# A fused attention and gated feed-forward kernel: two more warm-up products, later masks, small norm steps on GpSimd, and a new order table

## The chip, the cores and the metric

One core of one Trainium2 chip. The metric is device microseconds (us) of one execution, measured in repeated runs; a separate profiled execution gives the trace. All runs quoted are of the state that the records call fast, and a kernel is compared with the kernel before on the same chip in the same rounds. In what follows a "product" is one matmul instruction of TensorE, and "the clock" is the pace of TensorE, which is half or full here (427 or 216 ns for a product of 512 columns).

## The reference

Two blocks with pre-normalisation on x of 2048 x 1024, all in bf16:

```python
h  = x + A(layernorm(x))          # 32 heads of 32; q, k, v, o projections of 1024 x 1024
h2 = h + B(layernorm(h))          # gate and up 1024 x 3584, silu(gate) * up, down 3584 x 1024
# A runs over 4 segments of 512 rows: causal softmax inside a segment, mixed by sigmoid(beta)
# with a linear memory M, z that is carried from segment to segment:
o = g * (phi(q) @ M) / (phi(q) @ z + 1e-6) + (1 - g) * softmax(q k^T * scale + mask) @ v
M = M + phi(k)^T v ;  z = z + sum(phi(k))
```

## The kernel before

The program lists all operations with their data dependences, runs a model of the core over them, and emits each engine's instructions in the order that the model found. Where two operations are ready, class and place in the list decide; a table shifts these per "stage" (a counter that the code advances at each group of operations).

```python
SHIFT = { 0: (-19, 0), 1: (424, -1), 2: (293, 0),   # ... cut: 482 entries, the last one 491
          488: (-337, 0), 489: (-203, 1), 490: (159, -1), 491: (-10, 0), }
...
    def schedule(self):
        for o in ops:
            late, cls = SHIFT.get(o.unit, (0, 0))
            o.seq += late + 1e-6 * o.seq
            o.cls += cls
...
    def warm(self, n, deps=()):                       # n products of zeros, 512 columns each
        w = self.oT[0][:, 4, :]
        o = self.mms(gr, [(... self.oT[0][:, 4, 0:128], w, True, True, 512)] * n, 0, split=n)
        o.cost["pe"] *= 2
...
    def constants(self):
        self.dve_op(lambda e: e.memset(w, 0.0), 300.0, [], [w], 0)
        self.warm(10)
        ...                                           # cut: identity, ones
        P(lambda e: e.memset(b, 0.0), 128, [], [b], 3)        # masks: 2 on GpSimd
        P(lambda e: e.memset(hm, 0.0), 4, [], [hm], 3)
        for j in range(4):                                    # and 8 on the vector engine
            self.dve_op(lambda e, bj=bj: e.memset(bj, 1.0), 180, [], [bj], 3)
            self.dve_op(lambda e, hj=hj: e.memset(hj, 1.0), 150, [], [hj], 3)
...
    def first_tile(self, t):                          # t = 0..3; odd tiles: sums on ScalarE
        var, mean, op = self.ln_act(t, x) if t % 2 else self.ln_stats(
            t, x, 1, (self.applied,) if t else ())
        self.dve_op(lambda e: e.tensor_scalar(ve, var, self.EPS, None, op0=ALU.add), ...)
        self.g.op("pool", 570.0, ... e.tensor_tensor(rs, ve, mh, op=ALU.pow) ...)
        for b in range(2):                            # two half tiles
            self.applied = self.dve_op(... e.tensor_scalar(xb, xb, mean, rs, op0=op, op1=ALU.mult) ...)
            self.transposes(...)                      # 4 products with the identity, TensorE
            self.evac(gr, out, ..., engs=("dve", "act"))      # out of PSUM, into xnT
...
    def first_half(self):     # loads, in this order: x tiles 0, 1; half of wq; x tiles 2, 3; half of wk; ...
        ...                   # then the four first_tile, then products of 128 columns per tile
```

The up-projection loads its weights in blocks of 512 KB into two pairs of buffers (w1b, w3b); a block's load starts when TensorE has read the block two before it.

The softmax here doesn't subtract the row's maximum and nothing guards it: scores larger than these inputs give would overflow.

## Time and profile before

| | us |
|---|---|
| first three runs | 906.48, 907.34, 907.40 |
| profiled run (span) | 905.84 (904.1) |
| all 37 runs of this study, several chips and calls | mean 906.4, from 904.5 to 909.8 |

In a page, line 1 of each part is the busy time of an engine. In the list of waits a row is "who waited <- for whom: us in total, times, longest". In the timeline a row is start, length, engine, line, operation, tiles and shapes, count, and in brackets the idle time just before it with what ended it. TensorE is busy 99% of the span, so only its idle time and its pace are to be won. The lines stand in the prediction.

### The profile page before, as it was taken

The numbers are of one execution on the slowest core, as the hardware profiler recorded it, in microseconds if no ns is written. First come the engines' busy times: TensorE is split into PE (matmuls) and PEld (weight loads), VectorE is DVE, ScalarE is ACT, GpSimd is POOL, SyncE is SP. The second block draws the span as 40 slices with busy tenths as digits, with TensorE's granted clock in tenths as the row PEclk, the third lists the DMA queues.
The fourth block names the chain that finished last, engine by engine and source line by source line (L and its number), as shares of the span: only waits on it lengthen the run. The fifth ranks groups of instructions, "written<-read, shape, count | busy, mean of one in ns | idle before, by whom it ended". The sixth has DMA issues, their size and how long they took to land.

```text
span 904.1 us, 12979 instructions
## 1 busy us (share of the span) xinstructions
PE 897.7 (99%) x5559; PEld 409.7 (45%) x5559; DVE 427.7 (47%) x653; ACT 284.5 (31%) x303; POOL 186.7 (21%) x246
## 2 busy tenths in 40 slices
PE   8999999999999999999999999999999999999998
PEld 6444444434444344444444444444444444444445
DVE  5667749688785765545434222201343333431111
ACT  5767757685866721111111110000121111110000
POOL 2446537465562732000000000000000000000000
PEclk9999999999999999999999999999999999999999
DMA  7896962653551257455215022013123221301110
GB/s 236 207 242 191 246 153 79 164 163 86 151 115 48 77 198 224 93 155 139 70 59 163 24 72 68 24 47 94 47 76 93 70 61 56 94 24 41 36 40 30
DMA packets 146473, 96.27 MB, mean 106 GB/s; under 512 B 45424, under 2 KB 133616, under 8 KB 146416
## 3 DMA queue, kind: packets, MB, share of 16 engines
q1 hardware_dynamic: 146416, 95.45, 38.3%
q8 instruction: 44, 0.72, 0.3%
q14 instruction: 13, 0.11, 0.0%
HBM read 76.55 MB, written 8.39 MB: 94 GB/s over the span
## 4 chain that ended last, share of the span: by engine, by line
PE 97%; DMA 2%; DVE 0%; issue 0%; ACT 0%; POOL 0%; SPq 0%
PE ps L702 90%; PE ps L1076 4%; PE ps L1031 3%; DMA w3b<-in_B_w_dram 1%; DMA wp<-in_A_wq_dram 1%; DMA xs<-in_A_x_dram 0%; PE ps L714 0%; DVE lnst L825 0%; ACT xnT L725 0%; POOL rstd L852 0%; DVE xs L856 0%; DVE ob L1225 0%; DVE lnmv L828 0%; DVE lnve L850 0%; DVE blkmask L788 0%
## 5 line engine op out<-in xcount | busy, mean ns | idle before, releaser
L702 PE MATMUL ps<-hnT,w1b 128*128 128x512 bf16 x896 | 220.0, 379 | 0.0
L702 PE MATMUL ps<-hnT,w3b 128*128 128x512 bf16 x896 | 219.0, 379 | 0.9 <-DMA w3b<-in_B_w_dram 0.9
L1193 ACT ACTIVATE sg<-ps 128x512 bf16<-128x512 f32 x112 | 66.9, 597 | 426.5 <-PE ps L702 426.5
L702 PE MATMUL ps<-w2b,hm 128*128 128x512 bf16 (+1 forms) x924 | 198.2, 373 | 0.0
L1196 DVE SCALAR_TENSOR_TENSOR t<-sg,ps 128x512 bf16<-128x512 bf16 x112 | 76.8, 685 | 198.9 <-ACT sg L1193 198.5
L1043 ACT ACTIVATE et<-ps 128x2048 bf16<-128x2048 f32 x80 | 150.0, 1875 | 39.7 <-PE ps L1031 39.2
L702 PEld LDWEIGHTS ps<-w2b,hm 128*128 128x128 bf16 x924 | 90.4, 98 | 103.2
L702 PEld LDWEIGHTS ps<-hnT,w1b 128*128 128x128 bf16 x896 | 87.2, 98 | 105.7 <-issue 7.9
L702 PEld LDWEIGHTS ps<-hnT,w3b 128*128 128x128 bf16 x896 | 86.7, 98 | 106.8 <-DMA w3b<-in_B_w_dram 2.2
L1052 POOL TENSOR_SCALAR_AFFINE_SELECT et<-et 128x512 bf16<-128x512 bf16 x96 | 88.4, 927 | 81.7 <-ACT et L1043 81.6
L1201 DVE SCALAR_TENSOR_TENSOR hm<-t,ps 128x512 bf16<-128x512 bf16 x112 | 76.3, 685 | 43.3 <-PE ps L702 40.6
L1225 DVE TENSOR_TENSOR ob<-hr,ps 128x512 bf16<-128x512 bf16 (+1 forms) x33 | 22.0, 670 | 125.0 <-PE ps L702 125.0
L702 PE MATMUL ps<-wo,oT 128*128 128x512 bf16 x256 | 63.9, 380 | 0.0
L702 PE MATMUL ps<-xnT,wp 128*128 128x512 bf16 (+1 forms) x352 | 62.5, 326 | 0.7 <-ACT xnT L725 0.5
L702 PE MATMUL ps<-hnT,wp 128*128 128x512 bf16 x256 | 62.6, 380 | 0.0
L702 PEld LDWEIGHTS ps<-xnT,wp 128*128 128x128 bf16 x352 | 28.8, 100 | 26.6 <-issue 2.8
L835 POOL TENSOR_SCALAR lnve<-lnmv 128x1 f32<-128x1 f32 x28 | 6.3, 228 | 150.8 <-DVE lnmv L828 150.7
L702 PEld LDWEIGHTS ps<-wo,oT 128*128 128x128 bf16 x256 | 23.9, 98 | 29.4 <-issue 2.7
L702 PEld LDWEIGHTS ps<-hnT,wp 128*128 128x128 bf16 x256 | 23.3, 98 | 28.5 <-issue 3.8
L1130 DVE STREAM_TRANSPOSE R<-Rc 128x1024 f32<-128x1024 f32 (+1 forms) x32 | 34.7, 1096 | 0.1
L1135 POOL TENSOR_TENSOR R<-Nsb,R 128x512 f32<-128x512 f32 x20 | 26.7, 1341 | 34.9 <-DVE R L1130 26.7
L1165 DVE TENSOR_TENSOR h<-h,ps 128x512 bf16<-128x512 bf16 x32 | 21.9, 684 | 24.8 <-PE ps L702 24.7
(85 smaller groups left out, 594.3 us busy)
## 6 DMA issues: line engine op xcount, KB each, us to landing
w3b<-in_B_w_dram SPq DMA_DIRECT2D x28, 512.0 KB, 3.8
w1b<-in_B_w_dram SPq DMA_DIRECT2D x28, 512.0 KB, 3.8
wp<-in_A_wv_dram SPq DMA_DIRECT2D x8, 1024.0 KB, 5.3
wp<-in_A_wq_dram SPq DMA_DIRECT2D x7, 1024.0 KB, 5.1
wp<-in_A_wk_dram SPq DMA_DIRECT2D x7, 1024.0 KB, 6.0
w2b<-in_B_w_dram SPq DMA_DIRECT2D x7, 1024.0 KB, 6.2
xs<-in_A_x_dram SPq DMA_DIRECT2D x16, 256.0 KB, 5.6
h<-in_A_x_dram SPq DMA_DIRECT2D x16, 256.0 KB, 3.7
```

Source lines behind the costliest of these rows:

```text
L702: return [e.matmul(p[0](gr), p[1], p[2], start=p[3], stop=p[4]) for p in part]
L1031: ins.append(e.matmul(self.bank(gr, j, 512 - 128 * kc, off), k[r, g0 + g, 128 * kc:128 * kc + 128], q[r, g0 + g, 128 * kc:512], start=True ...
L1043: return [e.activation(et[:, :, :], src, AF.Exp, scale=self.scale)]
L1052: self.pool_op(lambda e, v=v, pat=pat: e.affine_select(v, v, pattern=pat, compare_op=ALU.is_ge, fill=0.0, base=0, channel_multiplier=-1), ...
L1076: ins.append(e.matmul(self.ps[32 * j:32 * j + 32, b * 512 + 128 * kc:(b + 1) * 512], lhsT(i, kc, j), at[i, kc][:, j, :], start=kc == 0 and ...
L1130: sp = self.dve_op(lambda e, dst=dst, src=src: e.transpose(dst, src), dve_ns(512 * nr), [Rc[:, i, 0:nr, :]], [rs], 2)
L1135: self.either(lambda e, o1=o1, Ns=Ns, R0=R0: e.tensor_tensor(o1, Ns, R0, op=ALU.mult), 512, 2, [Ns, R0], [o1], 2)
L1165: self.g.op("dve", dve_ns(512), lambda e, gr, hs=hs: [e.tensor_tensor(hs, hs, self.bank(gr), op=ALU.add)], reads=[hs], writes=[hs], cls=1, ...
L1193: self.g.op("act", act_ns(512), lambda e, gr, sg=sg: [e.activation(sg, self.bank(gr), AF.Tanh, scale=0.5)], writes=[sg], cls=0, group=gg)
L1196: e.scalar_tensor_tensor(t1, sg, 1.0, self.bank(gr), op0=ALU.add, op1=ALU.mult)], reads=[sg], writes=[t1], cls=0,
L1201: e.scalar_tensor_tensor(dst, t1, 0.5, self.bank(gr), op0=ALU.mult, op1=ALU.mult)], reads=[t1], writes=[dst], cls=0,
L1225: self.g.op("dve", dve_ns(n), lambda e, gr, hs=hs, ob=ob, n=n: [e.tensor_tensor(ob, hs, self.bank(gr, 0, n), op=ALU.add)], reads=[hs], wri ...
```

## The change

Its intent: keep TensorE's clock from being half at the start, take small work out of the first tile's way, and a new order table that no longer touches stages from 444 on (the rest of the first half's up-projection, with one segment of the output projection between).

```diff
-SHIFT = { 0: (-19, 0), 1: (424, -1), ...  491: (-10, 0) }     # all values but one differ; cut
+SHIFT = { 0: (206, -1), 1: (232, 1), ...  443: (60, 0) }
-        self.warm(10)
+        self.warm(12)
-        (the ten mask memsets, moved out of constants)
+    def masks(self, on):                  # the same memsets, the two on GpSimd with deps=(on,)
+    ...
+        self.masks(self.applied[-1])      # called after the four first tiles
-            t, x, 1, (self.applied,) if t else ())
+            t, x, 1, (self.applied[0],) if t else ())
-        self.dve_op(lambda e: e.tensor_scalar(ve, var, self.EPS, None, op0=ALU.add), 70.0, [var], [ve], 0)
+        self.g.op("pool" if t % 2 else "dve", 230.0 if t % 2 else 150.0, lambda e, gr: [
+            e.tensor_scalar(ve, var, self.EPS, None, op0=ALU.add)], reads=[var], writes=[ve], cls=0)
-                                       290.0, [xb, mean, rs], [xb], 0, port=True)
+                                       370.0, [xb, mean, rs], [xb], 0, port=True))
```

The last pair only changes what the model assumes of that step's time, and so do two new numbers for the memsets that the cut hides.

## The prediction

> **What bounds the kernel now**
>
> I read the busy totals first, then who made TensorE wait, then the chain of waits, and last the first 15 us in order of time. The totals:
>
> ```profile
> span 904.1 us, 12979 instructions
> PE 897.7 (99%) x5559; PEld 409.7 (45%) x5559; DVE 427.7 (47%) x653; ACT 284.5 (31%) x303; POOL 186.7 (21%) x246
> ```
>
> TensorE (PE) is idle for 904.1 - 897.7 = 6.4 us in all; no other engine passes 47%. The page's row of granted clock is 9 (full) in all 40 slices, so no throttling enters. The view of waits, for TensorE's matmuls alone, lists nearly every idle stretch:
>
> ```profile
> PE ps L702 <- DVE oT L767: 1.2, 1, 1.2
> PE ps L714 <- DVE xs L856: 0.9, 1, 0.9
> PE ps L702 <- DMA w3b<-in_B_w_dram: 0.9, 2, 0.5
> PE ps L702 <- ACT xnT L725: 0.5, 1, 0.5
> PE ps L702 <- DMA wp<-in_A_wq_dram: 0.2, 1, 0.2
> ```
>
> They sum to 3.7 us; the other 2.6 us is the tail after the last product (the last DVE sum starts at 901.53). So 2.6 us of waiting sits in the first 11 us (1.2 + 0.9 + 0.5), 0.2 at 27 us, and 0.9 in two waits for up-projection weights, at 484 and 628 us. Everything between is a full TensorE, at a pace that the chain of waits gives (columns: start, length, what):
>
> ```profile
> 6.61 1.01 PE ps L714 x8
> 7.62 2.13 PE ps L702 x17
> 9.76 0.41 PE ps L714 x4
> 10.19 0.61 ACT xnT L725
> 10.84 2.41 PE ps L702 x40
> ...
> 326.81 152.07 PE ps L702 x704
> 478.90 5.49 DMA w3b<-in_B_w_dram
> 484.44 138.32 PE ps L702 x640
> ```
>
> 704 products of 512 columns in 152.07 us are 216 ns each; 640 in 138.32 us the same. There is nothing to win in that stretch except the waits. The reader should compare the second and the fifth row: 17 products take 2.13 us, one of 512 and sixteen of 128 columns; 40 products of 128 columns then take 2.41 us, 60 ns each. The timeline of the start shows it more plainly:
>
> ```profile
> 1.24 4.45 PE L702 MATMUL ps<-oT 128*128 128x512 bf16 x10 [1.24 <-DVE oT L767]
> 6.61 1.01 PE L714 MATMUL ps<-ident,xs 128*128 128x128 bf16 x8 [0.93 <-DVE xs L856]
> 7.42 0.63 PE L702 MATMUL ps<-oT 128*128 128x512 bf16 x1
> 7.84 1.91 PE L702 MATMUL ps<-xnT,wp 128*128 128x128 bf16 x16
> 9.55 0.83 PE L714 MATMUL ps<-ident,xs 128*128 128x128 bf16 x8
> 10.84 2.41 PE L702 MATMUL ps<-xnT,wp 128*128 128x128 bf16 x40 [0.47 <-ACT xnT L725]
> ```
>
> The ten warm-up products run at 445 ns each, twice 216; the sixteen products at 7.84 still at 119 ns each. TensorE is at half speed until about 10 us, although the warm-up exists to prevent that, and it has a hole of 0.93 us between warm-up and first transposes.
>
> **What the Trainium skill says**
>
> "TensorE: Matmul & The Clock Gate", section "Part 1: The HAM clock gate": the array starts at half clock and is released after about one busy window of 3.4 us; the window runs free of the kernel's start. The trace agrees with the two speeds (445 and 119 against 216 and 60 ns). It also fits that 4.45 us of warm-up was not enough here: a run of 4.45 us holds a whole 3.41 us window in only (4.45 - 3.41) / 3.41 = 30% of the phases, an estimate from the page's window.
>
> The same page, section "Back-to-back issue gap", gives N/2.4 + 2.5 ns, 216 ns at 512 columns, which the 152.07 us confirm; the 131 ns it also names for sustained streams is not seen here.
>
> "GPSIMD Engine Reference", section "3.1 Elementwise — side-by-side cycle accounting": an instruction there passes two software dispatch hops against one on the vector engine, so a tiny instruction should be dearer. It is: the same 128x1 addition has a median of 222 ns on GpSimd (28 of them) and 150 ns on the vector engine.
>
> **The change part by part**
>
> *Two more warm-up products.* At 427 ns each (4.45 us less about 0.2 us of the last one's drain, over 10; the weight loads start 427 ns apart too) they add 0.85 us. The stream then ends at 1.24 + 12 x 0.427 = 6.36 us instead of 5.5; the transposes start at 6.61, a little earlier after the next part. So the products lie in a hole and cost nothing, and TensorE is busy almost without a break from 1.24 to past 8 us. A busy run from 1.24 must hold a whole window by 1.24 + 2 x 3.41 = 8.1 us, so full clock comes at 4.7 to 8.1 us, not at about 10. Half-speed work from 6.61 to 10.17 is 3.56 us; at full speed up to 1.8 us of it goes. Not all reaches the path: the weight load at 7.78 ended a wait for the first half of wq, and the second x tile must be normalised by then.
>
> *Masks later.* Eight small memsets (four of 85 ns, four of 59 ns) leave the vector engine's first tile. Only two stand in the chain, with 0.04 us (mask at 4.79) and 0.10 us (at 5.09): 0.14 us gained. Two GpSimd memsets (0.28 and 0.10 us) move as well; nothing waited for them but these memsets. Their first readers start at 39.0 us, so building them after 13 us is safe.
>
> *Norm steps of odd tiles on GpSimd.* For tile 1 ScalarE's sums are done at 6.81 (6.62 + 0.19), but the addition on the vector engine starts at 7.58, behind a copy that waits for the transposes. The power then runs to 8.35. On GpSimd, idle there, it is 6.81 + 0.05 + 0.22 + 0.10 + 0.55 = 7.73: 0.6 us earlier. For tile 3 the sums end at 12.16; the addition (12.19) was not held up, and 0.22 replaces 0.15: about 0.1 us lost, or 0.3 if it queues behind tile 2's power (the pair fills GpSimd from 11.95 to 13.02).
>
> *Looser dependence.* The statistics of even tiles now follow the very first half-tile applied, not the latest one. Tile 2's, at 9.23 and 10.76 with a copy between, can come closer together: up to about 1 us for tile 2.
>
> *How much reaches TensorE's full stretch.* From 10.84 on TensorE has no wait until 27.4, so a gain must already stand there. If the sixteen products and the second transposes run at full speed, that is 16 x (119 - 60) = 0.9 us plus about 0.3 us. Against it: the first half of wk is issued at 3.67 and lands 7.0 us later, at 10.7, so wk products cannot start before that; now they start after 16 products of wq, 10.84 + 16 x 0.06 = 11.8. The limit gain is thus 1.1 us. Tile 3's data, held by ScalarE, leaves a similar slack. I take 0.7 us, estimated between 0.3 and 1.1.
>
> *The new order table.* It changes no work, only who goes first; entries from stage 444 on fall away. By counting stages in the code that is the up-projection from the end of the eighth column block of the first half, and one output-projection segment. It can remove or add waits such as those of 0.2 and 0.9 us. I count 0.3 us gained, with 1.3 us of spread either way.
>
> Sum: 907.3 - 0.7 - 0.3 = 906.3 us.
>
> **The rivals**
>
> *The wait moves to a transfer.* For: DMA is loaded at 0.81 and 0.91 in the first two stretches of 10 us, and the wq load at 21.02 takes 6.39 us and ended a 0.2 us wait at 27.46. Against: that load is issued when TensorE ends its last read of that buffer, so it moves forward with TensorE. If the loads do not move, the start's gain vanishes: 907.0.
>
> *The new order starves TensorE.* For: the model that orders the work does not know the real landing times; weight loads in the up-projection took 5.49 and 4.75 us at the two waits against a median of 3.8. Against: the old order had only 1.1 us of such waits. One bad order costs some waits of 0.5 to 1 us: 908 to 910.
>
> *The phase of the clock window rules.* The executions before are 906.48, 907.34 and 907.40, a split of 0.9 us, the size of the clock's loss at the start. If this is that luck, the change makes the lucky case the rule: 906.4 with less scatter, and nothing beyond.
>
> *The new order also cuts switches.* A group of row-tiled score products takes about 0.33 us against 0.21 of columns, 80 times, so some 10 us of switching exists. But each feeds its own exponential of 1.88 us from four banks, so groups stay apart; a few merged ones would give 905.
>
> **Range and chances**
>
> Start 0.7 with a spread of 0.4, order 0.3 with a spread of 1.3, chip noise 0.5: together about 1.5 us. I predict 906.3 us, 904.4 to 908.2 for 8 in 10. 2% is 18 us; only 6.4 us of idle time exists, so faster by over 2% gets 0.01; slower would need a bad order many times over, 0.01; within 2% gets 0.98.
>
> **What would show it right or wrong**
>
> Right: 12 warm-up products of about 5.3 us in a row, then transposes with an idle of under 0.3 us before them; the first sixteen products of 128 columns at about 60 ns; the small addition of tile 1 on GpSimd before 7.2 us; the stretch without waits beginning 0.3 to 1.1 us earlier; later waits of TensorE about 1 us in sum. Wrong: the sixteen still at 119 ns (more warm-up does not release the clock), a new wait for wk or the last x tile of the size of the gain, or waits for weights past 300 us of over 2 us, which would put the order table above everything else.

## The result

Six runs of the changed kernel: median 904.38 us (903.54 to 905.56); the kernel before beside it: 906.50 (905.70 to 907.40). The ratio is 0.9977, with a 95% interval of 0.9964 to 0.9989. A ratio here is the mean time of one kernel's fast runs over that of the other's of the same rounds, so not quite the ratio of the medians quoted. The class is "same" at 2%. The gain is 2.1 us.

The page of the changed kernel, its busy totals:

```profile
span 901.8 us, 13023 instructions
PE 896.5 (99%) x5561; PEld 408.8 (45%) x5561; DVE 423.8 (47%) x653; ACT 286.0 (32%) x306; POOL 179.9 (20%) x243
```

Its waits of TensorE, all of them:

```profile
PE ps L701 <- DVE oT L766: 1.2, 1, 1.2
PE ps L713 <- DVE xs L858: 1.1, 2, 0.7
PE ps L701 <- DVE lnve L853: 0.2, 1, 0.2
```

The three rows with DMA and ScalarE behind them (0.9, 0.5 and 0.2 us) are gone. The start, TensorE alone:

```profile
1.24 4.78 PE L701 MATMUL ps<-oT 128*128 128x512 bf16 x12 [1.24 <-DVE oT L766]
6.68 0.63 PE L713 MATMUL ps<-ident,xs 128*128 128x128 bf16 x8 [0.66 <-DVE xs L858]
7.15 0.38 PE L701 MATMUL ps<-oT 128*128 128x512 bf16 x1
7.67 1.05 PE L701 MATMUL ps<-xnT,wp 128*128 128x128 bf16 x16
9.21 0.72 PE L713 MATMUL ps<-ident,xs 128*128 128x128 bf16 x8 [0.48 <-DVE xs L858]
10.13 1.51 PE L701 MATMUL ps<-xnT,wp 128*128 128x128 bf16 x24 [0.20 <-DVE lnve L853]
```

The clock is full before the warm-up ends (12 products in 4.78 us, not 5.3), and the sixteen products take 1.05 us where they took 1.91. TensorE's stretch without a wait ("the stretch" below: the work that starts with the last row shown) begins at 10.13, 0.71 us earlier.

To divide the 2.3 us between the two spans I went through all matmuls of both traces and took from each start-to-start time what its columns need at full pace (columns over 2.4 ns, plus 2.5 ns; a quarter of it for products that use a quarter of the array). What is over is the surplus; a mode is a way to use the array, whole or in quarters:

```
us                                          before    after    difference
columns at full pace (2 more products)      873.46   873.89      +0.43
surplus in runs on the whole array (slow clock) 4.48   3.42      -1.06
surplus where TensorE was idle                3.59     2.14      -1.45
surplus at mode switches (178 and 176)       27.74    27.50      -0.24
surplus in runs of quarter products          -9.29    -9.27      +0.02
```

The last row is below zero because quarter products overlap more than this reckoning grants them; with it the rows add up to the 900.0 and 897.7 us from the first product to the last. Of the 1.45 us, 1.22 us lie after 326 us: 0.55 at the weight wait at 484 us and 0.67 at the one at 628 us; 0.39 are the wait at 27 us. So by this one pair of traces the first 28 us gave about 1 us and what comes after 326 us some 1.5; losses of 0.2 us in all lie scattered between. The experiments ask which of these is there in every execution.

### The profile page after: what moved, and what is told of

It is laid out like the page before. It is cut to its first block, busy times and chain, and to the rows that moved or that the text cites. A ratio compares the mean times of both kernels' runs of the same rounds, so it can differ in the third digit from the quotient of the medians.

```text
span 901.8 us, 13023 instructions
## 1 busy us (share of the span) xinstructions
PE 896.5 (99%) x5561; PEld 408.8 (45%) x5561; DVE 423.8 (47%) x653; ACT 286.0 (32%) x306; POOL 179.9 (20%) x243
## 4 chain that ended last, share of the span: by engine, by line
PE 99%; DMA 1%; DVE 0%; SPq 0%; issue 0%
PE ps L701 92%; PE ps L1080 4%; PE ps L1035 3%; DMA xs<-in_A_x_dram 1%; PE ps L713 0%; SPq L292 0%; DVE lnst L827 0%; DVE xnT L725 0%; DVE ob L1229 0%; DVE xs L858 0%; DVE lnve L853 0%
## 5 line engine op out<-in xcount | busy, mean ns | idle before, releaser
L1056 POOL TENSOR_SCALAR_AFFINE_SELECT et<-et 128x512 bf16<-128x512 bf16 x96 | 85.3, 895 | 86.8 <-ACT et L1047 79.7
L701 PE MATMUL ps<-wo,oT 128*128 128x512 bf16 x256 | 61.7, 379 | 0.0
L1035 PE MATMUL ps<-qT,kT 32*128 32x128 bf16 (+3 forms) x512 | 31.7, 301 | 0.0
L701 PE MATMUL ps<-wp,hnT 128*128 128x512 bf16 x128 | 31.3, 380 | 0.0
L701 PE MATMUL ps<-wp,xnT 128*128 128x512 bf16 x128 | 31.0, 380 | 0.0
```

Source lines behind the costliest of these rows:

```text
L701: return [e.matmul(p[0](gr), p[1], p[2], start=p[3], stop=p[4]) for p in part]
L1035: ins.append(e.matmul(self.bank(gr, j, 512 - 128 * kc, off), k[r, g0 + g, 128 * kc:128 * kc + 128], q[r, g0 + g, 128 * kc:512], start=True ...
L1056: self.pool_op(lambda e, v=v, pat=pat: e.affine_select(v, v, pattern=pat, compare_op=ALU.is_ge, fill=0.0, base=0, channel_multiplier=-1), ...
```

## The experiments

To change one thing and keep all else, most kernels below freeze the order: the model orders the program as it did, and only then are the named instructions moved or altered. I compared the instruction lists of each engine with the original's; for TensorE they differ in the warm-up count alone in experiments 2, 3, 4 and 7, by one swap alone in 11, and by both in 12. Two more kernels, the changed code with the old table and the changed code with the old entries from 444 on, could not be built and so never ran: the ordering model got stuck with 890 and 980 operations left. Some traces lack 80 to 100 matmul records; there the list of waits shows rows "<- issue" that are holes in the record, not waits.

Time that is the same in all executions of one order can be found by setting the ends of ScalarE's and the vector engine's evacuations of two traces against each other, one by one: the difference is flat and jumps where one of them waited. I call this the offset.

### 1 and 9. The changed kernel again

No edit.

> The changed kernel again, as the measure on this chip for the three beside it. Theory one (the gain has three parts: about 1 us at the start of which some is the clock's release, about 1.2 us of two waits for up-projection weights that are gone with the new order, 0.2 us of two mode switches fewer): ratio to the kernel before 0.9977, 2.1 us faster, between 1.5 and 2.7. Theory two (most of it is where the clock's window happens to lie): the gain on this chip may be anything from 0.8 to 3.5 us, since the two sets of three runs so far differ by that much.

> The changed kernel a third time, as the measure for the three beside it: 1.5 to 2.8 us faster than before. If the fourth x tile lands at time L in the trace, TensorE's full stretch begins at about L + 1.8 us (8.32 and 10.13, 8.90 and 10.79 in the two earlier profiles).

Measured: 904.05 us (903.52 to 904.89) against 906.22 (904.96 to 909.79), ratio 0.9971 (0.9956 to 0.9987); the third time 904.55 (904.01 to 905.11) against 905.42 (904.62 to 906.92), ratio 0.9990 (0.9977 to 1.0002). Over all 17 runs the changed kernel has a mean of 904.4 and a range of 2.0 us; the kernel before has 906.4 and 5.3 us over 37. It is not only faster but steadier (one source of the old scatter, a clock that falls back, is counted under "The clock's phase" below). Its stretch without waits began at 10.79 and 10.84 us, not at 10.13, with the clock full before 6.9 us in both: the 0.71 us of the first trace isn't there every time. The fourth x tile had landed at 8.90 and 8.95 us (8.32 in the first trace).

### 2, 5 and 10. The start's three parts on the old order

```diff
-        self.warm(10)
+        self.warm(10, made=12)        # 12 emitted; the model still counts 10
         self.g.schedule()
+        (the ten mask memsets go behind the last first-tile step;
+         the addition of tiles 1 and 3 goes from the vector engine to GpSimd)
```

> The kernel before with its order frozen, and only the start changed: 12 warm-up products, masks after the last first-tile step, the small addition of tiles 1 and 3 on GpSimd. Theory one: the start's share alone, 0.5 to 1.0 us faster than before, and the two weight waits of about 0.4 and 0.5 us still in the trace. Theory two: 0 to 1 us with the clock released early in the trace or not. Theory three (the order table is all; what the start gains is lost again at the first load of the next query weights): under 0.2 us faster, and the wait for that load near 27 us grows by what the start gained.

> The same kernel as the second experiment, once more. It came out 1.0 us slower than the one with 12 products alone when timed, but 0.6 us faster when profiled. If that is the scatter of one call to the next: here as fast as the kernel with 12 products within 0.5 us, or faster, and 0.9 to 1.8 us faster than before. If the later masks or the GpSimd steps cost something in most runs: again 0.7 to 1.2 us slower than the one with 12 products alone.

> Meant as the kernel before with both the start changed and its tail entries gone; the file given here is the one of the start alone, a third time, to set its scatter beside the changed kernel's on one chip. Full stretch at L + 1.7 us again; wait at 484 us between 0.3 and 1.3 us; 0.5 to 1.3 us faster than before and about 1.2 us slower than the changed kernel.

The tenth was meant to drop the tail entries too; I gave it the wrong file, and so it is a third run of the same kernel, whatever its name says. Measured: 905.55 (904.07 to 907.29), ratio 0.9991 (0.9973 to 1.0009); 905.55 (904.75 to 906.37), ratio 0.9988 (0.9976 to 1.0001); 904.88 (904.29 to 907.08), ratio 0.9997 (0.9984 to 1.0011). So 0.3 to 1.1 us faster than before, with 1 inside all three intervals, and with ranges of 1.6 to 3.2 us. In the second experiment's trace the gain is large: offset -1.27 us at 53 us. Here the first x tiles came early:

```profile
9.66 2.41 PE L702 MATMUL ps<-xnT,wp 128*128 128x128 bf16 x40 [0.37 <-ACT xnT L725]
```

In the fifth's trace, the same program with the clock full as early, the stretch begins at 10.86, and two waits carry it (TensorE's rows of the list of waits, the first two):

```profile
PE ps L702 <- ACT xnT L725: 1.4, 1, 1.4
PE ps L702 <- DMA w3b<-in_B_w_dram: 1.3, 1, 1.3
```

The first row explains the start. These are ScalarE's two instructions of the same trace that matter:

```profile
9.17 1.06 ACT L813 ACTIVATE oT<-xs 128x1024 bf16<-128x1024 bf16 x1 [1.07 <-DMA xs<-in_A_x_dram]
...
10.22 0.58 ACT L725 ACTIVATE xnT<-ps 128x512 bf16<-128x512 bf16 x1
```

Tile 1's eight transposes had ended at 9.41, but their evacuation starts at 10.22: in ScalarE's order it stands behind the first sum over tile 3 (9.17), and that one waits for tile 3 to land. So TensorE cannot go on before that landing, however fast its clock. In the kernel before the same two instructions start at 8.93 and 10.19; there the first four transposes, at half pace, ended only at 10.15, after the sum (9.99). All traces but those of experiments 11 and 12, sorted by order (clock: when the trace's record of the clock turns to full; landing: of the fourth x tile; stretch: its begin; difference: stretch less landing):

```
kernel                         products  clock full    landing  stretch  difference
before                            10     10.0             8.91    10.84     1.93
8  old order without tail         10     5.8              9.42    11.13     1.71
2  start parts                    12     6.7              7.94     9.66     1.72
5  start parts                    12     6.9              9.15    10.86     1.71
10 start parts                    12     6.1              7.97     9.72     1.75
4  12 products alone              12     5.7              8.39    10.11     1.72
6  12 products alone              12     7.1              9.24    10.95     1.71
changed                           12     5.4              8.32    10.13     1.81
1  changed                        12     6.9              8.90    10.79     1.89
9  changed                        12     6.8              8.95    10.84     1.89
7  new order, 10 products         10     10.1             8.26    10.79     2.53
3  new order, old start           10     4.6, lost at 8.0 7.75    10.63     2.88
```

In the old order, whenever the clock was full early, the stretch begins 1.71 to 1.75 us after the landing, with the masks and the GpSimd steps (2, 5, 10) or without (4, 6, 8). (In experiments 2 and 10 ScalarE came to the sum at 7.96 and 7.99 straight from the work before it, so a still earlier landing would have gained nothing there.) In the new order the chain is another, with nearly the same end: the vector engine takes tile 2's statistics ahead of the step on tile 1, and in experiments 1 and 9 these wait 0.60 and 0.66 us for the third x tile (landed 0.7 to 0.8 us before the fourth). So the masks and the GpSimd steps give the path nothing, although each does what it was meant to: from the first statistics to the first step on the data the first tile takes 2.41 us in the second experiment's trace and 2.55 in the fourth's (3.73 to 6.14; 3.70 to 6.25), and tile 1's step starts at 8.10 and 8.38. The late clock of the kernel before cost 0.2 us in its trace (1.93 against 1.71), and by this reading would have cost more with an early landing (no trace of that kernel shows one). The landing itself goes from 7.75 to 9.42 us over these traces, for the same loads in the same order.

### 4 and 6. Twelve products alone on the old order

```diff
-        self.warm(10)
+        self.warm(10, made=12)
```

> The kernel before with two more warm-up products emitted and nothing else, order frozen. Theory one: 0.3 to 0.6 us faster than before, first sixteen products at 56 ns each in the trace instead of 107, the second tile's transposes then waiting for the vector engine. Theory two: mean unchanged within 0.2 us where the old one already had an early release, less scatter between runs. A third outcome, no change and no early release, would say that the extra products do nothing.

> The kernel with 12 products alone, once more, beside the one before it. 0.8 to 1.6 us faster than the kernel before; offset against the kernel before in the trace -0.7 us at 27 us, -1.1 at 53 us, then only what the random landings of weights at 390 to 484 and 628 us give.

Measured: 904.60 (904.33 to 905.37), ratio 0.9977 (0.9962 to 0.9992), and 905.31 (904.56 to 906.27), ratio 0.9986 (0.9975 to 0.9998): 1.3 to 2.1 us faster than before, more than with all three parts. The sixth, in one call with the fifth, is only 0.2 us ahead of it, and both traces begin their stretch by the same rule, so I put the 1.0 us between experiments 2 and 4 to scatter; no run proves it. The clock was full by 7.1 us in all nine traces with 12 products, whatever the order of the loads, and by then in two of the five with 10.

### 7. Ten products on the new order

```diff
-        self.warm(12)
+        self.warm(12, made=10)
```

> The changed kernel with 10 products emitted in place of 12, order frozen. If the clock's release matters as predicted: 0.3 to 0.8 us slower than the changed kernel in the mean (1.3 to 1.8 us faster than before), with the sixteen products at 107 ns if the release comes after 9 us in the profiled run and 56 ns if it comes early. If the start is bound by the landing of the x tiles whatever the clock does: within 0.2 us of the changed kernel either way.

Measured: 904.26 us (904.10 to 904.90), ratio 0.9976 (0.9964 to 0.9988); the changed kernel's ratios were 0.9977, 0.9971 and 0.9990. The clock came late, at 10.1 us, and the products were slow:

```profile
6.70 1.01 PE L713 MATMUL ps<-ident,xs 128*128 128x128 bf16 x8 [1.02 <-DVE xs L858]
...
7.94 1.91 PE L701 MATMUL ps<-xnT,wp 128*128 128x128 bf16 x16
...
10.79 1.40 PE L701 MATMUL ps<-xnT,wp 128*128 128x128 bf16 x22 [0.30 <-DVE lnve L853]
```

Yet its stretch begins at 10.79, as early as experiment 1's with the clock full at 6.8, and its offset against the changed kernel is 0.66 us at 263 us, the same as experiment 1's. An early landing (8.26) and a late clock cost just what a late landing (8.90) and an early clock cost.

### 3. The new order with the old start

```diff
         self.g.schedule()         # of the changed kernel
+        (10 products; the memsets back between the first tile's steps;
+         the addition of tiles 1 and 3 back on the vector engine)
```

> The changed kernel with its order frozen and only the start put back: 10 warm-up products, masks between the first tile's steps, the small additions on the vector engine. Theory one: 1.0 to 1.6 us faster than the kernel before (weight waits gone, fewer switches), 0.5 to 1.0 us slower than the changed kernel. Theory three: as fast as the changed kernel within 0.3 us. Theory two: the trace shows whether the clock was released before or after 6 us, and the time follows that.

Measured: 904.28 us (903.98 to 904.99), ratio 0.9974 (0.9959 to 0.9989); the changed kernel 0.9971. So with the new order the whole start is worth some 0.2 us, less than the scatter of the runs, and the order alone gives nearly all of the gain. Its trace holds a surprise: the clock was full at 4.6 us and fell back.

```profile
1.24 3.96 PE L701 MATMUL ps<-oT 128*128 128x512 bf16 x10 [1.24 <-DVE oT L766]
6.86 0.63 PE L713 MATMUL ps<-ident,xs 128*128 128x128 bf16 x8 [1.67 <-DVE xs L862]
...
7.85 1.78 PE L701 MATMUL ps<-xnT,wp 128*128 128x128 bf16 x16
```

And the view by stretches, TensorE alone (the stretch, its length, busy time and count of products, granted clock, the DMA engines' share and GB/s):

```profile
7.00:8.00 1.00, 0.85 (x12) 0.99 1.07 326
8.00:9.00 1.00, 1.00 (x13) 0.50 1.17 316
```

Ten products took 3.96 us, the last one at full pace; after a hole of 1.67 us the transposes and the first two of the sixteen products still come at 55 ns; from 8.0 us to 11.4 they come at 107 ns again. The trace's record of the clock has it full for 3.41 us, from 4.57 to 7.98, and half for the next 3.41. That fits a window from 4.6 to 8.0 us which the hole left half empty (TensorE was busy for 47% of it); a threshold cannot be read from one such case, but all 14 traces together narrow it (last section).

### 8. The old order without its tail entries

```diff
-SHIFT = { ..., 443: (-5, 0), 444: (-58, -1), ..., 491: (-10, 0) }
+SHIFT = { ..., 443: (-5, 0) }
```

> The kernel before with the entries of its own order table from stage 444 on removed, nothing else; its order is the same up to the first blocks of the up-projection. If the wait for weights at 484 us comes from those entries: that wait is gone, 0.4 to 0.6 us faster than before, less scatter upwards, while the wait at 628 us (same order in all kernels) may still come or not. If it only moves: a wait of 0.3 to 0.6 us elsewhere between 400 and 550 us, and no gain.

Measured: 904.68 us (904.37 to 905.34), ratio 0.9981 (0.9969 to 0.9993), with a range of 1.0 us where the kernel before had 3.9. Its trace had the worst landing of all (9.42), and still its run took 904.50. TensorE's waits:

```profile
PE ps L1054 <- ACT xnT L1077: 1.6, 1, 1.6
PE ps L1054 <- DVE oT L1119: 1.2, 1, 1.2
PE ps L1066 <- DVE xs L1208: 1.1, 1, 1.1
PE ps L1054 <- DMA wp<-in_A_wq_dram: 0.4, 1, 0.4
```

No weight wait of the up-projection. This is where the old order placed it (the kernel before, 476 to 485 us, rows of TensorE and of the DMA queue):

```profile
477.17 2.09 SPq L293 DMA_DIRECT2D w3b<-in_B_w_dram  x2
...
479.76 1.29 SPq L293 DMA_DIRECT2D hr<-h_scr  x3
...
483.95 5.87 SPq L300 DMA_TRANSPOSE hnT<-hn  x2
484.44 2.76 PE L702 MATMUL ps<-hnT,w3b 128*128 128x512 bf16 x12 [0.39 <-DMA w3b<-in_B_w_dram]
```

The second w3b load starts at 478.90, when TensorE leaves the buffer, and is wanted 5.1 us later: 24 products of 216 ns lie between. In the six traces it takes 5.4 to 6.4 us, against a median of 3.8 to 4.0, with three loads of residual rows issued right behind it (that these slow it was not tested). Every trace of the old order has this wait, of 0.39, 0.34, 0.42, 1.29, 0.94 and 0.55 us (before and experiments 2, 4, 5, 6, 10; mean 0.66), as here in experiment 5:

```profile
485.39 2.76 PE L702 MATMUL ps<-hnT,w3b 128*128 128x512 bf16 x12 [1.29 <-DMA w3b<-in_B_w_dram]
```

Experiment 8 and all traces of the new order lack it: there a block is loaded 13 us before its use. (Other weight waits of the up-projection come and go: experiments 3, 7 and 12 of the new order show 0.2 to 0.4 us in all, between 300 and 413 us, and experiments 4 and 10 of the old 0.2 us each, at 395 and 466 us.) The wait at 628 us is another matter. The instructions around it are the same in both orders, the load had 4.3 us and took 4.75 in the trace of before; none of the other traces shows the wait. Those 0.67 us of the first comparison were luck.

### 11 and 12. The x tiles loaded first

```diff
         self.g.schedule()         # of the changed kernel
+        wq.start = x3.start + 0.001     # loads: x0, x1, x2, x3, then the half of wq
+        (tile 1's transposes ahead of the 16 products; tile 2's statistics ahead of tile 1's step)
```

Experiment 12 has 10 products besides.

> The changed kernel, order frozen but for the start: the third and fourth x tile are loaded ahead of the first half of wq, tile 1's transposes go ahead of the sixteen products, tile 2's statistics ahead of tile 1's step. If the landing of the x tiles is what bounds the start: x tiles landed by about 6 us, wq by 8.3 to 9.4, TensorE busy without a break from there, so 0.5 to 0.9 us faster than the changed kernel. If the total of bytes bounds it: a new wait for wk of about the same size, within 0.2 us of the changed kernel.

> The one before it with 10 warm-up products instead of 12. With the x tiles no longer in the way the clock should matter now and then: where the trace shows a release near 10 us, the products from about 8.9 us run at 107 ns and the kernel is 0.3 to 0.6 us slower than with 12; where it shows an early release, no difference.

Measured: 11: 903.87 us (903.82 to 905.32), ratio 0.9990 (0.9976 to 1.0003), the changed kernel beside it 0.9990 too; means 904.41 and 904.57. 12: 905.35 us (903.86 to 906.34), ratio 0.9997 (0.9984 to 1.0009). In the trace of 11 TensorE no longer waits for the fourth x tile. It waits 1.25 us for tile 1's normalised data, and then for bytes:

```profile
8.55 0.71 PE L713 MATMUL ps<-ident,xs 128*128 128x128 bf16 x8 [1.25 <-DVE xs L858]
9.10 1.28 PE L701 MATMUL ps<-xnT,wp 128*128 128x128 bf16 x20
10.75 1.29 PE L701 MATMUL ps<-xnT,wp 128*128 128x128 bf16 x20 [0.38 <-DMA wp<-in_A_wk_dram]
```

The half of wk lands at 10.71, and the stretch begins at 10.75. By the means the second branch of the expectation came out: no clear gain. But the five runs fall into two groups by their granted clock: 903.82 to 903.87 us at 1.000 (three), 905.22 and 905.32 at 0.998 (two), while the changed kernel beside it stood at 1.000 in all five, with 904.57. So the first branch may hold (0.7 us) where the clock does not fall back; five runs do not settle it. In 12 the clock came as late as 13.4 us, and with the x tiles out of the way this shows:

```profile
9.44 4.27 PE L701 MATMUL ps<-xnT,wp 128*128 128x128 bf16 x40
```

40 products in 4.27 us where the kernel before took 2.41; at 76 us its offset against the changed kernel is 2.06 us, that of 11 only 0.40. So a late clock does cost time where no landing covers it. By all its runs, no kernel here is clearly faster than the changed one.

## Why the prediction was right or wrong

The time, 904.38 us, lies on the lower edge of the range (904.4 to 908.2, centre 906.3). The direction and the class were right, but the gain was half of what came, 1.0 us against 2.1, and the shares were not right: 0.7 us for the start and 0.3 for the order, where in the runs the order alone gives nearly all of it. Part of the distance to the centre is the base: the sum starts from 907.3 us, the first three runs, and the kernel before has a mean of 906.4 over 37.

*What bounds the kernel.* Right: nothing but TensorE's idle time and pace changed, and the gain stayed far below the 6.4 us of idle time plus slow start. One reading was wrong on the way: a granted clock of full in all slices does not say that no half pace enters (last section); the prediction found the half pace in the products themselves.

*Two more products.* The mechanism was right. They filled the hole at no cost, and the clock is full by 7.1 us in every trace that has them, where ten left it to chance (4.6 to 13.4 us). What failed is the step "how much reaches TensorE's full stretch": 0.7 us, from the time saved on the sixteen products. I took the wk load as the limit and called tile 3's slack similar, but the nearer limit was the evacuation behind ScalarE's wait for tile 3, 1.71 us after its landing. For the kernel before's own landing (8.91) the clock was worth 0.2 us (1.93 less 1.71), and up to 1.2 us only in executions with a landing near 7.95 (10.84 less 9.66, an estimate). What I had named as a sign of being wrong, a new wait for the last x tile of the size of the gain, stands in the traces of the old order with a full clock and a late landing: 1.4 to 1.6 us in experiments 5, 6 and 8. With earlier landings it is 0.4 to 0.5 us, as before. Another sign named there, under 0.3 us of idle time before the first transposes, was met only where the clock came at 6.2 us or later; in the first trace it came at 5.4, the twelve products were done sooner, and 0.66 us of idle time stood behind them.

*Masks.* Predicted 0.14 us in the first tile's chain, measured 2.55 less 2.41, the same; on the path to the stretch, nothing.

*Norm steps.* Predicted 0.6 us earlier for tile 1. The result of the power came at 7.96 (7.39 + 0.57) in experiment 2, against 8.35, so 0.4 us; the step itself started 0.3 us earlier, and the path did not notice. GpSimd began the addition 0.08 us after the sums ended.

*The looser dependence.* In the changed kernel tile 2's statistics came at 7.55 and 8.16, close together as foreseen, but ahead of tile 1's step, which then waited behind them until 8.76, although its factor was ready at 7.93.

*The new order.* This is the term that was mis-sized: 0.3 us with a spread of 1.3. Experiment 3 gives it 2.4 us alone (0.0026 of 906.6), or 1.7 us when runs whose clock fell back are left out on both sides (905.98 less 904.24). Experiment 8 gives 1.7 us (0.0019 of 906.7; 1.8 with the same selection) for the dropped entries from 444 on alone, on the old start. The shares do not add up: on the old order twelve products alone gave 1.3 to 2.1 us, on the new order the whole start some 0.2. I read the 0.9 us of weight waits in one trace as the most that could be won. One of the two was a wait of every execution of that order, with a size from 0.3 to 1.3 us; the other was luck. The rival that the new order would starve TensorE did not come. Nor did the one that the start's gain is lost again at the wq load of 27 us: a wait for it comes and goes (0.2 to 0.4 us, before and in experiments 3, 6 and 9), and experiment 2, with the largest gain at the start, has none.

*The clock's phase.* I named the split of 0.9 us in the first three runs as possible luck of the clock; those three have no clock on record. The offsets show three sources of scatter: the landing of the fourth x tile (1.7 us from first to last), the weight wait at 484 us (1.0 us), and the clock, which in these traces shows only when the landing is early.

The runs without a trace say more of the clock than that. Each has its mean granted clock on record, and experiment 3's profiled run, with its one fall of 3.41 us, reads 0.998. Of 31 runs of the kernel before, 25 read 1.000, with a mean of 906.0 us; six read 0.998 or 0.996, with a mean of 907.7, and the three slowest of all (909.79, 908.92, 908.40) are among them. With 12 products in this load order none of 45 runs reads less than 1.000; with 10 it is eight of 48 (on the old order alone: none of 28 against seven of 37). So the two products also keep the clock from falling back, which the prediction lacks: by an estimate 0.3 us in the mean (six of 31 runs, times 1.7 us). When in those runs the clock fell, no trace shows.

Left open: how the 1.7 to 2.4 us of the order in timed runs divide beyond the traced wait at 484 us (mean 0.66 us) and two mode switches (0.24 us); only one run in each call was profiled, and the slow ones (up to 909.8 us) never were, so where their clock fell back is not known. Nor was the old order run with both the new start and the tail dropped.

## What to carry to other kernels

One trace is one execution: before a wait of half a microsecond is put on a list of gains, look whether the same instruction waits in several traces, and set the time that a load has against the time that it takes, because a load that just fits will wait in some runs. A faster clock or a step saved counts only at the place where the next stretch is released; follow that release back through the in-order engines to the transfer that stands behind it. When order and code change together, freeze the one to measure the other. And before runs are put to scatter, sort them by the clock that was granted to each.

## What the Trainium skill lacked or had wrong

- "TensorE: Matmul & The Clock Gate", section "Part 1: The HAM clock gate", gives the half clock after an idle window of about 3.4 us, and as the rule (in "HAM oscillation — how this bites in real kernels") no idle gaps above that. In experiment 3 a window with a hole of 1.67 us was enough: full at 4.6 us, half again from 8.0 to 11.4. And 4.45 us of warm-up with a hole of 0.93 us behind it left the clock at half until 10.0 in the kernel before. What share of a window must be busy is not told. An estimate from the 14 traces, with stretches of 3.41 us counted off in both directions from the release: the clock was released after stretches that were 92 to 100% busy, and not after those of up to 80%; once full it was kept through stretches of 54% and more, and lost after the one of 47%. Transposes are counted as busy in this: without them the stretch that released the clock in the kernel before would be 69% busy, less than the 74% of the one before it, which did not.
- The same page, section "Back-to-back issue gap", names 131 ns per product for sustained streams of 512 columns; here 704 of them take 152.07 us, 216 ns each, which is its formula.
- The same page names a throttle time among the metrics of a profile as the place to see a slow clock. The clock figure that these profiles carry, the mean granted clock, shows only half of it. The half pace before the first release is missing: it reads 1.000 for the kernel before, whose first 3.5 us of real work ran at half pace. A fall after the release is there: 0.998 in experiment 3, with 0.50 from 8 to 11 us.
- "DMA: Bandwidth & Descriptors" gives rates by size and, in "Latency and other measured facts", a latency that grows with the load on memory, but no spread from one execution to the next. The same loads in the same order landed the fourth x tile at 7.75 to 9.42 us, and a 512 KB load with a median of 3.8 to 4.0 us took 5.4 to 6.4 where three loads of 256 KB and a write were issued behind it.
- "GPSIMD Engine Reference", section "3.1 Elementwise — side-by-side cycle accounting", compares the two engines side by side at 2048 elements; for one element a partition the addition takes 0.22 us on GpSimd and 0.15 on the vector engine, and the power 0.57.
